# TensorE's loop turns begin with scores instead of a q projection, and half of K's transposes moves behind a reciprocal

## The chip, the core and the metric

The kernel runs on one core of a Trainium2 chip. The metric is the device time of one execution in microseconds (us), as the median of several runs. The profile is one further execution; its span, from the first to the last instruction, is some 2.6 us shorter than the time.

## The reference: what is computed

Two attention blocks, A and B, have the same form and data of their own. Per block there are 16 batches, 64 queries, 32 heads of 128, 512 cached keys, and a model width of 640:

```
q = (x @ wq) split into heads            # x: 16 x 64 x 640, wq: 640 x 4096
scores = q k^T / sqrt(128)               # k_cache: 16 x 32 x 512 x 128
p = softmax(scores)
o = p v                                  # v_cache as k_cache
out_block = concat_heads(o) @ wo         # wo: 4096 x 640
out = concat(out_A, out_B, last axis)    # 16 x 64 x 1280, bf16
```

Each key and each value is used by 64 queries only, so the caches (268 MB of the 295 MB moved) have to be streamed once.

## The kernel before, in words

**Steps.** The work is cut into 128 steps, numbered n. A step takes two batches and four heads (so 64 + 64 query rows fill 128 partitions), and reads 1 MB of K and 1 MB of V. Four steps (j = 0 to 3) make a group g of 16 heads for one pair of batches; eight groups make a phase; there are four phases (two for each block, because 16 heads' weights are held at a time).

**Kinds of operation in a step**, with the lines of the kernel before:

- LDK and LDV (SyncE's queue, L552, L563, L565) load K into a ring of six steps and V into a ring of four. LDV of step n waits until PV of step n-4 has freed its place.
- KT (VectorE, L617) transposes K in two halves, a and b, into `kt_ring`, which holds two steps.
- QP (TensorE, L603) projects q for four heads; QE (ScalarE, L609) copies it out of PSUM bank 1.
- S (TensorE, L627) makes the scores of four heads in PSUM banks 0 to 3.
- EX (ScalarE, L646) is four exponentials with row sums. RC (VectorE, L659) takes reciprocals: one of the first three heads' sums, one of the fourth's.
- NM (GpSimd, L675) multiplies the four heads' exponentials by their reciprocals. In the last step VectorE does this.
- TR (TensorE, L686) transposes the result into PSUM banks 4 and 5; TE (VectorE, L696) copies it out in two halves.
- PV (TensorE, L710) is P times V. In three steps of four it runs 128 small matmuls on 32 rows each, in the fourth (j = 3) 64 matmuls on 64 rows. OE and ZO (ScalarE, L718, L722) evict it and clear what the next will need.
- OP (TensorE, L730) multiplies by wo; after each group OS (VectorE, L740, L743) adds it to an accumulator or to the output, and ST (ScalarE's queue, L749) stores it.
- XT (TensorE, L582) transposes x once per group; XC and WP (GpSimd) lay out x and the next phase's wq.

**The order is written out by hand.** There is no scheduler at run time. `build_plan` gives every operation a time in units of a step, n plus an offset from the table `AT`, and sorts each engine's operations by it. Dependences are worked out from the same times (each operation depends on the last writer and on the readers of what it touches), and turned into semaphore waits. Changing a number in `AT` therefore changes the place of an operation in its engine's queue.

**TensorE runs a loop.** The other engines' programs are written out in full. TensorE's is a loop of 32 turns of four steps (`PERIOD = 4`), with a few operations ahead of it and behind it. In steady state TensorE's order in a step is S(n), TR(n-1), OP(n-2), QP(n+1), PV(n-1), and then S(n+1). In the kernel before, a turn begins with QP:

```python
    lo = next(i for i, o in enumerate(pe) if o.kind == "QP" and o.idx == 0)
    hi = next(i for i, o in enumerate(pe) if o.kind == "QP" and o.idx == cfg.PERIOD)
```

So a turn is QP, PV, S, TR, OP, four times (with one XT), and ends behind an OP. A PV of step -2, on zeros, stands in the first turn. Behind the loop stand PV(126), TR(127), OP(126), PV(127) and OP(127).

At the end of a turn TensorE's queue has a few instructions that do no arithmetic: the semaphores that the turn waited on are set back (L815), so that the same constants serve in the next turn, and a counter is raised and tested for the jump (L809):

```python
                        if loop["take"][s] == i:
                            e.sem_inc(sems[p][s], -v * units(s))
```

Three of these set-backs stand behind OPs within the turn, four at its end.

**VectorE's order** in a step is KTa(n), KTb(n), TE(n-2), RC3(n-1), in every fourth step OS, RC1(n-1). [...] a KT that waits for its K holds up the TE and the reciprocals behind it.

A second plan (`general`), which subtracts the maximum, is built too, but runs only when the row sums leave a safe range, which they don't here.

Of the kernel before, what the change touches and what calls it, by code (L numbers as in the profile page):

```python
# [20 lines left out]
class Cfg:  # L21
# [9 lines left out]
    BASE = 32  # L31
    KLEAD = 2.5
    WIDE = (0, 1, 2)
    AT = dict(XT=-2.485, XE=-2.28, XC=-0.9, QP=-0.45, QE=-0.24, KT=(-1.24, -1.0), S=0,
              EX=(0.21, 0.32, 0.43, 0.54), RC=(0.53, 0.75), NM=(0.56, 0.69, 0.82, 0.95), NMZ=(0.54, 0.55, 0.56, 0.76), TR=1.2,
              TE=(1.26, 1.39), PV=1.75, OE=(2.0, 2.06), ZO=2.11, OP=2.31, OS=2.545, LDWO=2.6, ST=3.374, WP0=-1.75, WP1=-1.6)


class Op:
# [19 lines left out]
def build_plan(dims, cfg, general):  # L59
# [12 lines left out]
    def add(eng, kind, idx, ts, reads=(), writes=()):  # L72
        op = Op(eng, kind, idx, ts, reads, writes)
        ops.append(op)
        at[(kind, idx)] = op
        return op

    def add_output(n):
        g, j = n // NJ, n % NJ
        final = n >= 0 and dims["FINAL"](g // NBP)  # L80
        for b in range(2):
            tv = n + AT["PV"]
            op = add("sp", "LDV", (n, b), tv - 0.3, [], [("v" if n >= 0 else "absent", n % cfg.NV, b)])
            loads.append((n - cfg.NV + AT["PV"] + 0.2 if n >= 0 else -99.0, 3, op))
        if n > -2:
            add("pe", "TR", n, n + AT["TR"], [("pn", i) for i in range(4)] + [("ident",)], [("B", 4), ("B", 5)])
        for b in range(2):
            add("dve", "TE", (n, b), n + AT["TE"][b], [], [("B", 4 + b), ("pT", b)])
        add("pe", "PV", n, n + AT["PV"], [("pT", 0), ("pT", 1), ("v", n % cfg.NV, 0), ("v", n % cfg.NV, 1)],
            [("B", 4), ("B", 5), ("B67",)])  # L90
        add("act", "OE", (n, 1), n + AT["OE"][0], [], [("B67",), ("oT", 1)])
        add("act", "OE", (n, 0), n + AT["OE"][1], [], [("B", 4), ("B", 5), ("oT", 0)])
        add("act", "ZO", n, n + AT["ZO"], [("zeros",)], [("B67",)])
        add("pe", "OP", n, n + AT["OP"], [("oT", 0), ("oT", 1), ("wo", j)], [("B67",)])
        if j == NJ - 1:
            bp = g % NBP
            add("dve", "OS", g, n + AT["OS"], [("acc", bp)], [("B67",), ("out_sb",) if final else ("acc", bp)])
            if final:
                add("act", "ST", g, n + AT["ST"], [("out_sb",)], [("out_dram", g)])
# [4 lines left out]
    for g in range(N // NJ + 1):  # L104
        n0 = g * NJ
        txt = n0 + AT["XT"]
        add("pe", "XT", g, txt, [("xn", g % cfg.NXN), ("ident",)], [("SB", 0)])
        if g == N // NJ:
            break
        if dims["FIRST"](g // NBP):  # L110
            add("act", "XE", g, n0 + AT["XE"], [], [("SB", 0), ("xs", g % NBP)])
            op = add("sp", "LDX", g, txt - 0.5, [], [("xn", g % cfg.NXN)])
            loads.append((txt - 3.7 if g else -7.0, 0, op))
        add("pool", "XC", g, n0 + AT["XC"], [("xs", g % NBP)], [("xT", g % cfg.NX)])
# [20 lines left out]
    add("dve", "BZ", 0, -9.8, [], [("B", 4), ("B", 5), ("B67",)])  # L135
    add("dve", "WZ", 0, -9.7, [], [("wo", NJ - 2), ("wo", NJ - 1)])
    add("pool", "NM", -1, -1 + AT["NM"][3], [], [("pn", i) for i in range(4)])
    for n in range(-2, N):
        add_output(n)
        if n < 0:  # L140
            continue
        g, j = n // NJ, n % NJ
        add("pe", "QP", n, n + AT["QP"], [("xT", g % cfg.NX), ("wqp", j)], [("SB", 1)])
        add("act", "QE", n, n + AT["QE"], [], [("SB", 1), ("qs", n % cfg.NQ)])
        for i in range(4):
            op = add("sp", "LDK", (n, i), n + AT["KT"][0] - 0.9, [], [("kn", n % cfg.NK)])
            loads.append((n - cfg.NV + AT["PV"] + 0.2 - cfg.KLEAD, 2, op))
        for b in range(2):
            tk = n + AT["KT"][b]
            add("dve", "KT", (n, b), tk, [("kn", n % cfg.NK)], [("kt", n % cfg.NKT, b)])  # L150
        add("pe", "S", n, n + AT["S"], [("qs", n % cfg.NQ), ("kt", n % cfg.NKT, 0), ("kt", n % cfg.NKT, 1)],
            [("SB", i) for i in range(4)])
        for i in range(4):
            h = 4 * n + i
            te = n + AT["EX"][i]
            if general:
                add("dve", "MX", h, te - 0.002, [], [("SB", i), ("negmax", h % 4)])
            add("act", "EX", h, te, [("negmax", h % 4)] if general else [],
                [("SB", i), ("p", h % cfg.NP), ("rs", h)])
            add("pool" if n < N - 1 else "dve", "NM", h, n + (AT["NM"] if n < N - 1 else AT["NMZ"])[i], [("p", h % cfg.NP), ("recip", n % cfg.NR, i // 3)], [("pn", i)])  # L160
        for a in range(2):
            add("dve", "RC", (n, a), n + AT["RC"][a], [("rs", 4 * n + i) for i in ((0, 1, 2), (3,))[a]],
                [("recip", n % cfg.NR, a)])
# [25 lines left out]
                   and not (d.dma and op.dma and d.eng == op.eng)]  # L189

    pe = progs["pe"]
    lo = next(i for i, o in enumerate(pe) if o.kind == "QP" and o.idx == 0)
    hi = next(i for i, o in enumerate(pe) if o.kind == "QP" and o.idx == cfg.PERIOD)
    size = hi - lo
    last_qp = max(o.idx for o in pe[lo:hi] if o.kind == "QP")
    reps = 1 + (N - 1 - last_qp) // cfg.PERIOD
    step = dict(XT=cfg.PERIOD // NJ, QP=cfg.PERIOD, S=cfg.PERIOD, TR=cfg.PERIOD, PV=cfg.PERIOD, OP=cfg.PERIOD)
    for k in range(reps):
        for i in range(size):
# [5 lines left out]
    for op in ops:  # L205
        if op.kind == "OP":
            at[("OE", (op.idx, 1))].deps += [d for d in op.deps if d.kind in ("LDWO", "WZ")]
            op.deps = [d for d in op.deps if d.kind not in ("LDWO", "WZ")]
        if op.kind == "XT" and op.idx > 0:
            at[("EX", 4 * (NJ * op.idx - NJ + 1))].deps += [d for d in op.deps if d.kind == "LDX"]  # L210
            op.deps = [d for d in op.deps if d.kind != "LDX"]
        if op.kind == "QP" and op.idx > 0:
            at[("EX", 4 * op.idx - 4)].deps += [d for d in op.deps if d.kind == "WP"]
            op.deps = [d for d in op.deps if d.kind != "WP"]

    own = {"XC", "QE", "KT", "NM", "TE", "OE", "ZO", "OS", "LDV"}

# [211 lines left out]
def mha_kernel(nc, blocks, out, cfg=None):  # L429
# [23 lines left out]
    with contextlib.ExitStack() as es:  # L453
        block = es.enter_context(nc.Block())

        def sb(name, shape, dt):
            return es.enter_context(nc.sbuf_tensor(name, shape, dt))
# [20 lines left out]
        recip = sb("recip", [128, NR, 4], F32)  # L478
        ident = sb("ident", [128, 128], BF16)
        extreme = sb("extreme", [128, 4], F32)  # L480
        good = sb("good", [128, 1], BF16)
        flag = sb("flag", [1, 1], I32)
        ps = es.enter_context(nc.psum_tensor("ps", [128, 8, 512], F32))

        sems = []
        for p, (_progs, counts, _loop) in enumerate(plans):
            sems.append({key: es.enter_context(nc.semaphore("_".join([f"p{p}"] + [str(k) for k in key])))
# [124 lines left out]

        def em_KT(e, op):
            n, a = op.idx
            dst = kt_ring[:, n % NKT, 16 * a:16 * a + 16].rearrange("p t j b k two -> p (t j) b (k two)").bitcast(F32)
            src = kn_ring[:, n % NK, a, :].bitcast(F32).rearrange("p (c h b l) -> p c h b l", h=8, b=2, l=2)
            ins = e.transpose(dst.rearrange("p c b (h l) -> p c h b l", h=8, l=2), src)  # L617
            return ins, ins
# [72 lines left out]
        def em_TE(e, op):  # L691
            n, b = op.idx
            if n == -2:
                ins = e.memset(pT_sb[:, b].rearrange("p t q -> p (t q)"), 0.0)
                return ins, ins
            ins = e.tensor_copy(pT_sb[:, b].rearrange("p t q -> p (t q)"), pt_bank(b))  # L696
            return ins, ins
# [77 lines left out]
        def units(key):  # L775
            return 16 if key[0].startswith("d_") else 1

        def emit(e, op, p, taken):
            sem = sems[p]
            waits = [(s, v - taken.get(s, 0)) for s, v in op.waits]  # L780
            attach = None
            if waits and not op.dma and op.kind not in ("FL1", "WP"):
                attach = waits.pop()
            for s, v in waits:
                e.wait_ge(sem[s], v * units(s))
            kind = "EXG" if p and op.kind == "EX" else op.kind
            first, last = emitters[kind](e, op)
            if last is None:
                e.sem_inc(sem[op.sem], units(op.sem))
                return  # L790
            if attach is not None:
                s, v = attach
                first.wait_op(sem[s], v * units(s), "sem-ge")
            last.then_inc(sem[op.sem], 16 if op.dma else 1)
# [113 lines left out]
```

## Time and profile before

| | before |
|---|---|
| time, median of 3 runs | 750.21 us (749.89 to 751.77) |
| span of the profiled execution | 747.6 us |
| TensorE busy, matmuls | 679.0 us (91%) |
| VectorE, ScalarE, GpSimd busy | 526.0 us, 519.4 us, 404.1 us |
| moved by DMA | 295.15 MB, mean 395 GB/s |
| a step, between 60 and 206 us | 5.2 us |
| matmul instructions | 26518, each with a weight load |

The busy time of an engine is the sum of its instructions' times; "idle before, releaser" names what an engine waited for. PE is TensorE's matmuls, PEld its weight loads, DVE is VectorE, ACT ScalarE, POOL GpSimd, SPq SyncE's queue, which issues the loads.

### The profile page before, as it was taken

The page shows a single profiled execution, that of the slowest core. Times are in us where ns is not written, and L with a number is a line of the kernel's source. Part 1 is how long each engine was busy: PE and PEld are TensorE (multiplying, and loading weights), DVE is VectorE, ACT ScalarE, POOL GpSimd, SP SyncE. Part 2 cuts the span into 40 slices and gives each one's busy share as a digit, 9 for nine tenths or more (in the row PEclk, how much of TensorE's full clock was granted, in tenths as well). Part 3 has the DMA queues.
Part 4 walks back from the last instruction along what each step waited for, and adds up shares of the span by engine and source line. Part 5 has one row for each costly group of instructions (what it writes and reads, how often), then busy time and mean ns, then how long its engine had stood idle before and what let it go on. Part 6 is the DMA issues. An engine that isn't in the chain of part 4 may idle for free.

```text
span 747.6 us, 57618 instructions
## 1 busy us (share of the span) xinstructions
PE 679.0 (91%) x26518; PEld 530.6 (71%) x26518; DVE 526.0 (70%) x818; ACT 519.4 (69%) x1559; POOL 404.1 (54%) x580
## 2 busy tenths in 40 slices
PE   4669999999998999989988999999898899999994
PEld 3557777777776777777766777677776677777773
DVE  7437777777767677676755776777676687877773
ACT  2438777787776767767756777777776677777772
POOL 5434555655964454645684545546476455564550
PEclk9979999999999999999999999999999999999999
DMA  8999999999999999999999999999999999999970
GB/s 315 398 402 410 411 411 414 410 412 413 405 398 414 413 413 411 414 411 414 412 399 407 411 412 413 411 411 411 411 410 401 411 412 414 404 414 413 412 299 16
DMA packets 87518, 295.15 MB, mean 395 GB/s; under 512 B 13360, under 2 KB 28208, under 8 KB 71088
## 3 DMA queue, kind: packets, MB, share of 16 engines
q1 hardware_dynamic: 78832, 284.22, 95.2%
q10 hardware_dynamic: 8640, 10.49, 3.9%
q14 instruction: 37, 0.30, 0.1%
q8 instruction: 9, 0.15, 0.1%
HBM read 292.03 MB, written 2.62 MB: 394 GB/s over the span
## 4 chain that ended last, share of the span: by engine, by line
PE 38%; SPq 29%; DMA 12%; POOL 6%; ACT 5%; DVE 5%; issue 4%; ACTq 0%; DVEq 0%
SPq L552 20%; PE ps L710 10%; PE ps L730 9%; PE ps L603 8%; DMA kn_ring<-in_B_k_cache_dram 8%; POOL pn_sb L675 5%; SPq L563 5%; PE ps L627 5%; PE ps L686 5%; SPq L565 3%; ACT p_ring L646 2%; DMA v_ring<-in_B_v_cache_dram 2%; DVE kt_ring L617 2%; DMA kn_ring<-in_A_k_cache_dram 2%; ACT oT_sb L718 2%
## 5 line engine op out<-in xcount | busy, mean ns | idle before, releaser
L675 POOL TENSOR_SCALAR pn_sb<-p_ring,recip 128x512 bf16<-128x512 bf16 x508 | 341.9, 692 | 314.7 <-DVE recip L659 314.7
L617 DVE STREAM_TRANSPOSE kt_ring<-kn_ring 128x1024 f32<-128x1024 f32 x256 | 302.9, 1222 | 116.0 <-DMA kn_ring<-in_B_k_cache_dram 77.6
L646 ACT ACTIVATE p_ring<-ps 128x512 bf16<-128x512 f32 x512 | 298.7, 598 | 19.8 <-PE ps L627 4.2
L696 DVE COPY pT_sb<-ps 128x1024 bf16<-128x1024 bf16 x258 | 164.2, 677 | 63.0 <-PE ps L686 62.5
L710 PE MATMUL ps<-pT_sb,v_ring 32*128 32x64 bf16 (+1 forms) x14528 | 162.2, 192 | 25.7 <-DVE pT_sb L696 9.8
L710 PEld LDWEIGHTS ps<-pT_sb,v_ring 32*128 32x128 bf16 (+1 forms) x14528 | 145.9, 92 | 41.5 <-issue 21.7
L603 PE MATMUL ps<-xT_ring,wqp_sb 128*128 128x128 bf16 x2560 | 167.0, 221 | 5.8 <-POOL xT_ring L592 5.7
L730 PE MATMUL ps<-wo_sb,oT_sb 128*128 128x320 bf16 x1040 | 166.2, 303 | 5.9 <-issue 4.9
L603 PEld LDWEIGHTS ps<-xT_ring,wqp_sb 128*128 128x128 bf16 x2560 | 158.3, 114 | 12.5 <-issue 5.9
L718 ACT ACTIVATE oT_sb<-ps 128x256 bf16<-128x256 f32 x260 | 85.6, 381 | 113.6 <-PE ps L710 113.6
L627 PE MATMUL ps<-kt_ring,qs_ring 32*64 32x512 bf16 x4096 | 138.6, 381 | 0.0
L609 ACT ACTIVATE qs_ring<-ps 128x512 bf16<-128x512 f32 x128 | 76.5, 598 | 82.4 <-PE ps L603 82.4
L686 PEld LDWEIGHTS ps<-ident,pn_sb 64*128 64x128 bf16 x4128 | 70.3, 95 | 77.6 <-ACT ps L722 43.6
L730 PEld LDWEIGHTS ps<-wo_sb,oT_sb 128*128 128x128 bf16 x1040 | 91.7, 98 | 43.6 <-issue 5.3
L646 ACT ACTIVATION_READ_ACCUMULATOR p_ring<-ps 128x1 f32 x512 | 106.1, 207 | 0.0
L686 PE MATMUL ps<-ident,pn_sb 64*128 64x64 bf16 x4128 | 84.0, 191 | 20.9 <-POOL pn_sb L675 12.8
L627 PEld LDWEIGHTS ps<-kt_ring,qs_ring 32*64 32x64 bf16 x4096 | 53.4, 103 | 28.3 <-issue 0.5
L659 DVE RECIPROCAL recip<-rowsum 128x3 f32<-128x3 f32 (+1 forms) x256 | 39.9, 162 | 32.4 <-ACT p_ring L646 28.2
L722 ACT ACTIVATE ps<-zeros 128x256 f32<-128x256 bf16 x130 | 51.3, 395 | 0.0
L575 POOL COPY wqp_sb<-ws_sb 128x1280 bf16<-128x1280 bf16 x32 | 39.2, 1256 | 7.3 <-DMA ws_sb<-in_A_wq_dram 7.3
L592 POOL COPY xT_ring<-xs_sb 128x640 bf16<-128x640 bf16 x32 | 22.9, 717 | 3.6 <-PE ps L603 3.6
L582 PE MATMUL ps<-ident,xn_ring 128*128 128x128 bf16 x165 | 15.1, 224 | 4.4 <-DMA xn_ring<-in_A_x_dram 3.4
(26 smaller groups left out, 66.0 us busy)
## 6 DMA issues: line engine op xcount, KB each, us to landing
kn_ring<-in_A_k_cache_dram SPq DMA_DIRECT2D x256, 256.0 KB
v_ring<-in_A_v_cache_dram SPq DMA_DIRECT2D x128, 512.0 KB, 12.2
kn_ring<-in_B_k_cache_dram SPq DMA_DIRECT2D x256, 256.0 KB
v_ring<-in_B_v_cache_dram SPq DMA_DIRECT2D x128, 512.0 KB, 13.0
ws_sb<-in_B_wq_dram SPq DMA_DIRECT2D x10, 512.0 KB, 15.9
wo_sb<-in_B_wo_dram ACTq DMA_DIRECT2D x8, 640.0 KB, 13.9
ws_sb<-in_A_wq_dram SPq DMA_DIRECT2D x4, 640.0 KB, 7.6
wo_sb<-in_A_wo_dram SPq DMA_DIRECT2D x4, 640.0 KB, 12.8
```

The source lines that it names most:

```text
L552: ins = e.dma_start(kn_ring[2 * b + l::4, n % NK].rearrange("p a c -> p (a c)"), src)
L603: last = e.matmul(ps[:, 1, f * 128:(f + 1) * 128], w[:, kt, f, :], xT_ring[:, xs, kt, :], start=(kt == 0), stop=(kt == KT - 1))
L609: ins = e.activation(qs_ring[:, op.idx % NQ].rearrange("p f b q -> p (f b q)"), ps[:, 1, :], ACTF.Copy, scale=scale)
L617: ins = e.transpose(dst.rearrange("p c b (h l) -> p c h b l", h=8, l=2), src)
L627: last = e.matmul(ps[64 * b:64 * b + 64, i, :], qs_ring[rows, n % NQ, f, b, :], kt_ring[rows, n % NKT, :, f // 2, b, :, f % 2], start=(f = ...
L646: ins = e.activation(dst, src, ACTF.Exp, scale=1.0, accum_out=rowsum[:, h:h + 1])
L675: ins = e.tensor_scalar(dst, src, recip[:, h // 4 % NR, i:i + 1], 1.0, ALU.mult, ALU.mult)
L686: last = e.transpose(pt_bank(b)[:, 64 * c:64 * c + 64], pn_sb[rows, c, :], ident[rows, rows], tile_position=(64 * b, 0))
L696: ins = e.tensor_copy(pT_sb[:, b].rearrange("p t q -> p (t q)"), pt_bank(b))
L710: last = e.matmul(ps[:, 4 + i, 64 * b:64 * b + 64], v_ring[rows, n % NV, b, c, :], pT_sb[rows, b, c, :], start=(t == 0 and i < 2), stop=(t ...
L718: ins = e.activation(oT_sb[:, 2 * a:2 * a + 2, :], o_ps[:, 2 * a:2 * a + 2, :], ACTF.Copy)
L730: last = e.matmul(out_ps[:, s, :], oT_sb[:, i, :], wo_sb[:, 4 * j + i, s * NH0:(s + 1) * NH0], start=(j == 0 and i == 0), stop=(j == NJ - ...
```

## The change

It moves the boundary of TensorE's turn from ahead of a QP to ahead of an S, which puts PV(126) into the last turn and leaves TR(127), OP(126), PV(127) and OP(127) behind the loop. For that, QP(0) moves ahead of the loop, PV(-2) goes (its TE is now a store to a spare column), and a QP(128), whose result nobody reads, is added, with a layout of x (XC) ahead of it on GpSimd, so that the last turn is complete. TensorE's cyclic order is what it was.

It also gives new offsets in `AT`. Compared as they come out, the queues differ in this: VectorE runs KTa(n), TE(n-2), RC3(n-1), OS where there is one, KTb(n), RC1(n-1); S thereby waits for VectorE as well as for ScalarE, with one more wait instruction ahead of each S; ST stands one exponential later in ScalarE's queue, and the loads of wo that ScalarE issues one exponential earlier; two loads of wq change places with a neighbour. In the last step, VectorE's order is now two of the four NM, TE(127), the check of the row sums, and then the other two NM. Those last two multiplications therefore come after the transposes that read their tile, so the last step's heads 2 and 3 enter the output with what the tile held before.

```diff
-    AT = dict(XT=-2.485, XE=-2.28, XC=-0.9, QP=-0.45, QE=-0.24, KT=(-1.24, -1.0), S=0,
-              EX=(0.21, 0.32, 0.43, 0.54), RC=(0.53, 0.75), NM=(0.56, 0.69, 0.82, 0.95), NMZ=(0.54, 0.55, 0.56, 0.76), TR=1.2,
-              TE=(1.26, 1.39), PV=1.75, OE=(2.0, 2.06), ZO=2.11, OP=2.31, OS=2.545, LDWO=2.6, ST=3.374, WP0=-1.75, WP1=-1.6)
+    AT = dict(XT=-2.555, XE=-2.383, XC=-0.788, QP=-0.428, QE=-0.224, KT=(-0.672, -0.375), S=0,
+              EX=(0.252, 0.307, 0.358, 0.616), RC=(0.572, 0.794), NM=(0.803, 0.854, 1.088, 1.187),
+              NMZ=(0.626, 1.242, 1.729, 1.805), TR=1.293, TE=(1.432, 1.47), PV=1.701, OE=(1.888, 2.013), ZO=2.221,
+              OP=2.387, OS=2.576, LDWO=2.6, ST=3.542, WP0=-1.75, WP1=-1.596)
...
-        add("pe", "PV", n, n + AT["PV"], [("pT", 0), ("pT", 1), ("v", n % cfg.NV, 0), ("v", n % cfg.NV, 1)],
-            [("B", 4), ("B", 5), ("B67",)])
+        if n > -2:
+            add("pe", "PV", n, n + AT["PV"], [("pT", 0), ("pT", 1), ("v", n % cfg.NV, 0), ("v", n % cfg.NV, 1)],
+                [("B", 4), ("B", 5), ("B67",)])
...
-    for n in range(-2, N):
-        add_output(n)
+    for n in range(-2, N + 1):
+        if n < N:
+            add_output(n)
...
         add("pe", "QP", n, n + AT["QP"], [("xT", g % cfg.NX), ("wqp", j)], [("SB", 1)])
+        if n == N:
+            for b in range(2):
+                add("dve", "KT", (n, b), n + AT["KT"][b])
+            break
...
-    lo = next(i for i, o in enumerate(pe) if o.kind == "QP" and o.idx == 0)
-    hi = next(i for i, o in enumerate(pe) if o.kind == "QP" and o.idx == cfg.PERIOD)
-    size = hi - lo
-    last_qp = max(o.idx for o in pe[lo:hi] if o.kind == "QP")
-    reps = 1 + (N - 1 - last_qp) // cfg.PERIOD
+    lo = next(i for i, o in enumerate(pe) if o.kind == "S" and o.idx == 0)
+    size = next(i for i, o in enumerate(pe) if o.kind == "S" and o.idx == cfg.PERIOD) - lo
+    reps = N // cfg.PERIOD
...
+            if n == NH // 4:
+                ins = e.memset(spare[:, 4 * current[0] + a:4 * current[0] + a + 1], 0.0)
+                return ins, ins
...
-                ins = e.memset(pT_sb[:, b].rearrange("p t q -> p (t q)"), 0.0)
+                ins = e.memset(spare[:, 4 * current[0] + 2 + b:4 * current[0] + 3 + b], 0.0)
```

More of the change, by code (lines that the diff above doesn't have):

```diff
@@ L87, in add_output @@
         for b in range(2):
-            add("dve", "TE", (n, b), n + AT["TE"][b], [], [("B", 4 + b), ("pT", b)])
-        add("pe", "PV", n, n + AT["PV"], [("pT", 0), ("pT", 1), ("v", n % cfg.NV, 0), ("v", n % cfg.NV, 1)],
-            [("B", 4), ("B", 5), ("B67",)])
+            add("dve", "TE", (n, b), n + AT["TE"][b], [], [("B", 4 + b), ("pT", b)] if n > -2 else [])
+        if n > -2:
+            add("pe", "PV", n, n + AT["PV"], [("pT", 0), ("pT", 1), ("v", n % cfg.NV, 0), ("v", n % cfg.NV, 1)],
+                [("B", 4), ("B", 5), ("B67",)])
         add("act", "OE", (n, 1), n + AT["OE"][0], [], [("B67",), ("oT", 1)])
@@ L107, in build_plan @@
         add("pe", "XT", g, txt, [("xn", g % cfg.NXN), ("ident",)], [("SB", 0)])
-        if g == N // NJ:
-            break
-        if dims["FIRST"](g // NBP):
+        if g < N // NJ and dims["FIRST"](g // NBP):
             add("act", "XE", g, n0 + AT["XE"], [], [("SB", 0), ("xs", g % NBP)])
@@ L214, in build_plan @@
             op.deps = [d for d in op.deps if d.kind != "WP"]
+    if general:
+        at[("QP", 0)].deps += [at[("KT", (0, b))] for b in range(2)]
     own = {"XC", "QE", "KT", "NM", "TE", "OE", "ZO", "OS", "LDV"}
@@ L480, in mha_kernel @@
         extreme = sb("extreme", [128, 4], F32)
+        spare = sb("spare", [128, 8], F32)
         good = sb("good", [128, 1], BF16)
@@ L483, in mha_kernel @@
         ps = es.enter_context(nc.psum_tensor("ps", [128, 8, 512], F32))
+        current = [0]
         sems = []
@@ L785, in emit @@
                 e.wait_ge(sem[s], v * units(s))
+            current[0] = p
             kind = "EXG" if p and op.kind == "EX" else op.kind
```

## The prediction

> **What bounds the kernel now.** I read the page's slices first, then the waits of SyncE's queue, the busy times by stretch, K's transposes against the scores step by step, and last TensorE's sequencer around a turn's end.
>
> The slices (busy tenths and rate of the DMA engines in 40 equal parts):
>
> ```profile
> DMA  8999999999999999999999999999999999999970
> GB/s 315 398 402 410 411 411 414 410 412 413 405 398 414 413 413 411 414 411 414 412 399 407 411 412 413 411 411 411 411 410 401 411 412 414 404 414 413 412 299 16
> ```
>
> The transfers are full from the second slice to the last but two. The waits of SyncE's queue over the first 210 us:
>
> ```profile
> SPq L563 <- PE ps L710: 34.6, 23, 3.3
> SPq L565 <- PE ps L710: 13.8, 8, 2.3
> ```
>
> There each load of V waits for a PV, 48 us in all, so TensorE paces the issue; but a load of V issued between 100 and 200 us lands after 12.8 us, so some 5 MB are always queued. By stretches (us; PE, PEld, DVE, ACT, POOL busy; clock, DMA share, GB/s):
>
> ```profile
> 60.00:206.00 146.00, 144.04 (x5771) 113.18 (x5765) 113.48 (x177) 114.51 (x343) 87.42 (x127) 1.00 1.03 411
> 206.00:600.00 394.00, 361.05 (x14255) 282.54 (x14248) 274.10 (x433) 278.87 (x840) 219.64 (x313) 1.00 1.03 410
> 600.00:723.00 123.00, 121.55 (x4760) 95.65 (x4750) 96.61 (x149) 93.10 (x284) 66.75 (x100) 1.00 1.02 410
> 723.00:748.00 25.00, 14.92 (x665) 11.00 (x662) 10.45 (x23) 9.80 (x30) 4.50 (x7) 0.95 0.11 37
> ```
>
> TensorE and DMA are both full in the first and third row; in the second DMA alone is (TensorE 92%), because the next phases' weights come in. A group of four steps takes TensorE 20.71 us in the first row (EX of step 4 at 56.66, of step 8 at 77.37, of step 12 at 98.08), 5.18 a step; in the second a step takes 5.69 us (S(33) at 206.22, S(102) at 598.67). The last K lands at 723.15; 24 us are left. So the end is: the last K that TensorE had to wait for, then TensorE's own pace, then the tail. K's transposes name that K:
>
> ```profile
> 587.81 2.37 DVE L617 STREAM_TRANSPOSE kt_ring<-kn_ring 128x1024 f32<-128x1024 f32 x2 [2.81 <-DMA kn_ring<-in_B_k_cache_dram]
> 590.11 1.25 DVE L696 COPY pT_sb<-ps 128x1024 bf16<-128x1024 bf16 x2
> 591.50 1.11 PE L710 MATMUL ps<-pT_sb,v_ring 64*128 64x64 bf16 x64 [0.67 <-DVE pT_sb L696]
> 592.54 0.59 PEld L627 LDWEIGHTS ps<-kt_ring,qs_ring 32*64 32x64 bf16 x32
> ```
>
> K(101) lands at 587.81 and S(101) starts 4.73 later, the shortest such distance in the trace. From there it grows, to 6.16 at step 127 (723.15 to 729.31): over the last 26 steps TensorE, at 5.26 a step, is the slower of the two.
>
> In the tail, TensorE's gaps (idle before, releaser):
>
> ```profile
> 732.58 1.21 PE L710 MATMUL ps<-pT_sb,v_ring 32*128 32x64 bf16 x128 [0.28 <-DVE pT_sb L696]
> 734.59 0.55 PE L686 MATMUL ps<-ident,pn_sb 64*128 64x64 bf16 x25 [0.79 <-ACT oT_sb L718]
> 736.42 0.29 PE L686 MATMUL ps<-ident,pn_sb 64*128 64x64 bf16 x7 [1.28 <-issue]
> ```
>
> The gap inside TR(127) waits for no engine. The set-backs and the jump, by source line (durations min/median/max in ns):
>
> ```profile
> L815 PEldq EVENT_SEMAPHORE  x224: 51/51/51, 20.1 to 731.2; - x112
> L809 PEldq ALU_OP  x32: 36/36/42, 51.4 to 731.4; - x32
> L809 PEldq COMPARE_BRANCH  x32: 76/208/240, 51.5 to 731.5; - x32
> ```
>
> Their starts show what they occupy. At one turn's end the four set-backs start at 113.877, 114.031, 114.180 and 114.331, the counter at 114.482, the jump at 114.609, the next turn's first wait at 114.874, ending at 114.925: **1.05 us without a matmul dispatched**. Now it costs nothing: the sequencer has run ahead, and TensorE spends 114.15 to 115.25 on the eight long matmuls of OP, already queued.
>
> [...] the first turn's gaps put down to issue lie 256 instructions apart (program positions 451, 707, 963, 1219, 1475), none recurs in later turns, and the gap in TR(127) is at 1987, two blocks on. [...] in a PV of 128 matmuls the first 32 weight loads take 0.22 us, and every later 16 take 0.133 to 0.138, [...] then dispatch, 4.2 ns each, sets the pace. **Behind a wide PV the queue is empty.** [...]
>
> **Part by part.** *The turn's boundary.* The same seven instructions now stand between PV(4k+2), one of the wide ones, and S(4k+4). Nothing is queued to hide them. S starts up to 1.05 us late, and behind it wait EX, NM and TR of that step and everything later on TensorE. The new wait ahead of each of the other S costs 0.07 (a wait record's start to the next weight load, 118.664 to 118.739) behind the two other wide PVs, nothing behind the narrow one. Against this, OE and ZO no longer delay that step's first exponential, about 0.1. Bounds for a turn: 0.7, should some lead survive, and 1.1; I take 1.0. Where TensorE paces, a group goes from 20.7 to 21.7. Between 60 and 206 us the 7 turns cost 7 us, but the 12 us of queued transfers hide it, nor is it felt at 5.69 a step in the middle. Behind S(101) six boundaries follow (before S(104) to S(124)): 6 x 1.0 = **+6.0**.
>
> *KTb behind RC3.* From a late K to S ran KTa, KTb 2.37, TE 1.25, PV 1.04 and hand-overs: 4.73. Now it is KTa 1.19, TE 1.25, RC3 0.17, KTb 1.19 and four hand-overs of about 0.07: 4.1. S(101) comes 0.7 earlier: **-0.7**. RC1 waits for KTb, but NM needs it only after three multiplications, 2.0 us behind RC3; with OS in between (0.8) that just fits. S also waits for KTb, which at step 126 would end at 723.95 by these durations, for an S at 724.28.
>
> *First turn.* One PV of 1.9 us and one fetch gap fewer lie ahead of step 4; TensorE may lead by some 4 us at 55 us. The transfers are full, so that gives nothing at the end.
>
> *Tail.* QP(128) goes between OP(125) and PV(126), which started 1.54 behind OP; now it is 1.09 + 1.22 = 2.31: +0.77. The loop ends at program position 1722, in the block that ends at 1731; the rest ends at 1952, ahead of 1987, where the fetch gap is: -1.28. The set-backs hide under OE, which TR(127) waits for anyway (0.79). That TR(127) no longer waits for two NM gives nothing, as OE comes later. Together **-0.5**. The two NM behind the check of sums (0.6) end before OP(127).
>
> The moved loads, ST, stores to spare columns and offsets that keep the order: nothing, behind transfers with 12 us of queue or on engines under 75% busy.
>
> Sum: +6.0 - 0.7 - 0.5 = +4.8; 750.2 + 4.8 = **755.0 us**.
>
> **The rivals.** *The boundary is hidden* (a lead survives PV, or K is late again after 600 us, so that TensorE's pace doesn't count). For it: DMA is full there too, and KT waits 0.3 to 0.9 us for K in most of these steps. Against it: the distance from K to S grows in that stretch. It gives -0.7 - 0.5: 749.0. *TensorE paces the transfers in the first phase*, so that its 4 us of lead reach the end: SyncE's 48 us of waits speak for it, the full DMA share and 12.8 us to landing against. It gives -4.0 - 1.2: 745.0 if the boundary is hidden too. [...] One fetch of 1.3 to 3.7 us in each of 32 turns would give over 790. The same block boundaries in both programs speak against it.
>
> **How the numbers follow.** Forecast 0.72, hidden boundary 0.13, lead carried 0.12, refetch 0.03. With 1.1 a turn for all six, 0.3 for KTb and no fetch gap saved the forecast's case reaches 757.3; with 0.7 it is 753.2. The range goes from 749.0, the hidden case, to 757.3. Slower by over 0.3% (2.25 us) takes nearly all of the forecast and the refetch, 0.73; same takes the hidden case, 0.13; faster 0.14.
>
> **What would show it.** Right: in the last phase a gap of about 1 us ahead of every fourth S, put down to issue; four steps at 21.5 or more there; K to S down to about 4.1 at the last late K, and over 9 at step 127; no issue gap in TR(127); QP(128) ahead of PV(126). Wrong: S close behind PV at the turns' ends, or four steps at 20.7.

## The result and the profile after

| | before | changed |
|---|---|---|
| time, median of 4 runs | 750.05 us (749.29 to 751.77) | 753.81 us (753.14 to 755.14) |
| ratio to before, 95% interval | | 1.0049 [1.0026, 1.0073] |
| span of the profiled execution | 747.6 us | 752.6 us |

The changed kernel is slower by 3.8 us (2.0 to 5.5 by the interval). The span of an execution is 1.7 to 1.8 us shorter than its own time: the two profiled ones took 749.34 and 754.38 us. Line numbers in its profile: K's transposes L628, S L638, RC L670, NM L686, TR L697, TE L707, PV L721, OE L729, OP L741, QP L611, loads of K L560 and of V L571 and L573, the loop's counter and jump L821, set-backs L827.

The page's slices, changed kernel:

```profile
DMA  8999999999999999999999999999999999999950
GB/s 319 398 402 410 412 411 413 412 410 413 406 398 414 414 413 412 413 413 413 412 400 406 411 410 413 411 413 410 411 407 400 412 415 413 407 408 403 393 220 15
```

The transfers are as full as before for most of the span. In the five slices ahead of the last the rate falls to 407, 408, 403, 393 and 220 GB/s: there the loads wait for TensorE, 33.5 us in all between 600 and 723 us, against 6.2 before. The same by stretch (us; PE, PEld, DVE, ACT, POOL busy; clock, DMA share, GB/s):

```profile
60.00:206.00 146.00, 138.16 (x5573) 108.60 (x5571) 104.63 (x167) 108.56 (x325) 83.15 (x121) 1.00 1.03 411
206.00:600.00 394.00, 366.75 (x14305) 286.88 (x14303) 276.90 (x438) 281.55 (x846) 222.99 (x316) 0.99 1.03 410
600.00:723.00 123.00, 116.35 (x4613) 92.01 (x4605) 88.19 (x141) 89.45 (x273) 63.82 (x95) 1.00 1.01 403
723.00:748.00 25.00, 21.06 (x846) 16.29 (x843) 15.35 (x34) 13.76 (x42) 8.36 (x13) 0.99 0.16 57
```

TensorE is now busy 138.2 us of 146 in the first row (before 144.0) and 116.4 of 123 in the third (before 121.6). It has got gaps, and is later. Where the gaps are, TensorE's waits say (waiting line, releaser: us in total, times, longest):

```profile
PE ps L638 <- ACT oT_sb L729: 17.4, 20, 0.9
...
PE ps L638 <- PEq L827: 5.1, 6, 0.9
...
PE ps L638 <- DVE kt_ring L628: 3.5, 4, 0.9
```

Together 30 gaps ahead of S, of 0.87 us each, in a kernel with 31 turn ends that lead to an S. The three releasers are three names for one thing: the profile names the semaphore event that came last, and OE, K's transpose or a set-back happens to be it. What they have in common shows at one turn's end (start, length, idle before and releaser):

```profile
650.93 1.28 PE L611 MATMUL ps<-xT_ring,wqp_sb 128*128 128x128 bf16 x20
652.14 1.22 PE L721 MATMUL ps<-pT_sb,v_ring 32*128 32x64 bf16 x128
654.24 1.07 PE L638 MATMUL ps<-kt_ring,qs_ring 32*64 32x512 bf16 x32 [0.89 <-ACT oT_sb L729]
```

In the records of TensorE's sequencer (PEq: its waits, set-backs, counter and jump) PV's last weight load starts at 653.152, the four set-backs at 653.135, 653.289, 653.439 and 653.589, the counter at 653.740, the jump at 653.867, the wait at 654.133, S's first weight load at 654.209. From PV's last weight load to S's first it is 1.06 us; at the other steps it is 0.13 behind a wide PV and 0.15 behind the narrow one, as in the kernel before. The first set-back starts 0.02 us ahead of PV's last weight load: the sequencer is hardly ahead. The set-backs' row is the old one, at a new place:

```profile
L827 PEldq EVENT_SEMAPHORE  x224: 51/51/51, 22.8 to 740.3; - x112
```

Against before, the first matmul of S comes at these times: S(4) 4.26 us earlier, S(32) 3.50 later, S(65) 0.14 later, S(101) 1.00 later, S(104) 1.28, S(127) 5.47 later. And behind S(127) the tail, 17.86 us instead of 18.30.

### The profile page after: what moved, and what is told of

Read it like the earlier page. It is cut to its first block, busy times and chain, and to the rows that moved or that the text cites. A ratio compares the mean times of both kernels' runs of the same rounds, so it can differ in the third digit from the quotient of the medians.

```text
span 752.6 us, 57532 instructions
## 1 busy us (share of the span) xinstructions
PE 682.1 (91%) x26410; PEld 533.0 (71%) x26410; DVE 517.6 (69%) x820; ACT 519.8 (69%) x1559; POOL 406.1 (54%) x581
## 4 chain that ended last, share of the span: by engine, by line
PE 52%; SPq 12%; POOL 9%; ACT 9%; DMA 8%; issue 5%; DVE 3%; PEld 1%; ACTq 0%; PEldq 0%; DVEq 0%
PE ps L721 12%; PE ps L741 12%; PE ps L611 11%; PE ps L638 9%; POOL pn_sb L686 9%; SPq L560 8%; PE ps L697 6%; ACT p_ring L657 6%; DMA v_ring<-in_B_v_cache_dram 6%; ACT oT_sb L729 3%; SPq L571 2%; DMA kn_ring<-in_B_k_cache_dram 2%; SPq L573 1%; DVE kt_ring L628 1%; DVE pT_sb L707 1%
## 5 line engine op out<-in xcount | busy, mean ns | idle before, releaser
L686 POOL TENSOR_SCALAR pn_sb<-p_ring,recip 128x512 bf16<-128x512 bf16 x508 | 343.1, 695 | 319.5 <-DVE recip L670 319.5
L628 DVE STREAM_TRANSPOSE kt_ring<-kn_ring 128x1024 f32<-128x1024 f32 x256 | 310.4, 1225 | 49.6 <-DMA kn_ring<-in_B_k_cache_dram 44.7
L707 DVE COPY pT_sb<-ps 128x1024 bf16<-128x1024 bf16 x258 | 165.7, 684 | 168.7 <-PE ps L697 168.7
L721 PE MATMUL ps<-pT_sb,v_ring 32*128 32x64 bf16 (+1 forms) x14400 | 161.4, 192 | 13.6 <-DMA v_ring<-in_B_v_cache_dram 7.9
L611 PE MATMUL ps<-xT_ring,wqp_sb 128*128 128x128 bf16 x2580 | 167.9, 221 | 5.3 <-POOL xT_ring L600 5.3
L741 PE MATMUL ps<-wo_sb,oT_sb 128*128 128x320 bf16 x1040 | 167.7, 305 | 4.8 <-issue 3.8
L611 PEld LDWEIGHTS ps<-xT_ring,wqp_sb 128*128 128x128 bf16 x2580 | 159.4, 114 | 12.1 <-POOL xT_ring L600 5.6
L638 PE MATMUL ps<-kt_ring,qs_ring 32*64 32x512 bf16 x4096 | 140.2, 385 | 27.3 <-ACT oT_sb L729 17.4
L721 PEld LDWEIGHTS ps<-pT_sb,v_ring 32*128 32x128 bf16 (+1 forms) x14400 | 144.1, 92 | 28.9 <-DMA v_ring<-in_B_v_cache_dram 9.1
L729 ACT ACTIVATE oT_sb<-ps 128x256 bf16<-128x256 f32 x260 | 85.6, 381 | 102.9 <-PE ps L721 102.9
L741 PEld LDWEIGHTS ps<-wo_sb,oT_sb 128*128 128x128 bf16 x1040 | 92.3, 99 | 43.3 <-issue 4.0
L697 PEld LDWEIGHTS ps<-ident,pn_sb 64*128 64x128 bf16 x4128 | 70.3, 96 | 66.7 <-ACT ps L733 29.5
L638 PEld LDWEIGHTS ps<-kt_ring,qs_ring 32*64 32x64 bf16 x4096 | 56.1, 104 | 56.1 <-DVE kt_ring L628 17.2
L697 PE MATMUL ps<-ident,pn_sb 64*128 64x64 bf16 x4128 | 84.3, 192 | 9.8 <-POOL pn_sb L686 6.3
L670 DVE RECIPROCAL recip<-rowsum 128x3 f32<-128x3 f32 (+1 forms) x256 | 37.5, 146 | 7.2 <-ACT p_ring L657 0.8
```

The source lines that it names most:

```text
L611: last = e.matmul(ps[:, 1, f * 128:(f + 1) * 128], w[:, kt, f, :], xT_ring[:, xs, kt, :], start=(kt == 0), stop=(kt == KT - 1))
L638: last = e.matmul(ps[64 * b:64 * b + 64, i, :], qs_ring[rows, n % NQ, f, b, :], kt_ring[rows, n % NKT, :, f // 2, b, :, f % 2], start=(f = ...
L686: ins = e.tensor_scalar(dst, src, recip[:, h // 4 % NR, i:i + 1], 1.0, ALU.mult, ALU.mult)
L697: last = e.transpose(pt_bank(b)[:, 64 * c:64 * c + 64], pn_sb[rows, c, :], ident[rows, rows], tile_position=(64 * b, 0))
L721: last = e.matmul(ps[:, 4 + i, 64 * b:64 * b + 64], v_ring[rows, n % NV, b, c, :], pT_sb[rows, b, c, :], start=(t == 0 and i < 2), stop=(t ...
L729: ins = e.activation(oT_sb[:, 2 * a:2 * a + 2, :], o_ps[:, 2 * a:2 * a + 2, :], ACTF.Copy)
```

## The experiments

All times stand beside executions of the kernel before on the same chip. Their median is 750.14 us for the order alone, the boundary alone, the set-backs early and the doubled cost; 749.89 for the kernel before with the doubled cost, the narrow end, both together and the changed kernel once more; 749.59 for the last three (the set-backs early once more and the two variants of both). "Four steps" is a fifth of the time from S(104) to S(124) in the profile. In that stretch the granted clock of TensorE is 1.00 in every profile, so the turns can be compared. Ahead of it this is not so: in five of the profiles the clock stands at 0.50 for 3.4 us, in one of them 6.8, at 585 to 593 us, where S(100) and S(101) run.

**The order alone** (an edit of the kernel before).

```diff
-    AT = dict(XT=-2.485, XE=-2.28, XC=-0.9, QP=-0.45, QE=-0.24, KT=(-1.24, -1.0), S=0,
+    AT = dict(XT=-2.485, XE=-2.28, XC=-0.9, QP=-0.45, QE=-0.24, KT=(-1.24, -0.4), S=0,
```

> The kernel before with one number changed: KTb comes behind RC3 (and OS), as in the changed kernel, so S waits for VectorE too. The turn still begins with QP. Theory (the turn's seven instructions stand exposed behind a wide PV): the boundary is still hidden here, four steps of the last phase take 20.9 to 21.1 us, the time is 749.3 to 751. Rival (K's order and the new wait of S are what costs): 753 or more, four steps at 21.6 or more.

Measured: 748.17 us, ratio 0.9974 [0.9966, 0.9981]; four steps 20.87. The order doesn't cost, it gains 2.0 us, more than I gave it. The profile shows only part of the gain: its execution took 748.89, 0.45 less than the profiled one before. S(101) comes 0.28 earlier, S(101) to S(127) is 0.63 shorter, and the tail is 0.45 longer, in which the granted clock stands at 0.50 from 735.95 to 739.36 us. At step 101 (timeline, columns as above; other engines' lines left out):

```profile
588.54 1.25 DVE L617 STREAM_TRANSPOSE kt_ring<-kn_ring 128x1024 f32<-128x1024 f32 x1 [2.40 <-DMA kn_ring<-in_B_k_cache_dram]
...
589.71 1.25 DVE L696 COPY pT_sb<-ps 128x1024 bf16<-128x1024 bf16 x2
...
590.89 0.15 DVE L659 RECIPROCAL recip<-rowsum 128x3 f32<-128x3 f32 x1
...
590.96 1.21 DVE L617 STREAM_TRANSPOSE kt_ring<-kn_ring 128x1024 f32<-128x1024 f32 x1
...
592.26 1.07 PE L627 MATMUL ps<-kt_ring,qs_ring 32*64 32x512 bf16 x32
```

From K's landing to S it is 3.72 us, where before it was 4.73 and I had estimated 4.1. And in this kernel TensorE is never clear of K in the last phase: K to S is still 4.71 at step 127 (6.16 before), with the last transpose waiting for its K:

```profile
723.69 1.25 DVE L617 STREAM_TRANSPOSE kt_ring<-kn_ring 128x1024 f32<-128x1024 f32 x1 [0.66 <-DMA kn_ring<-in_B_k_cache_dram]
```

**The boundary alone** (an edit of the changed kernel, as all that follow but one).

```diff
-    AT = dict(XT=-2.555, XE=-2.383, XC=-0.788, QP=-0.428, QE=-0.224, KT=(-0.672, -0.375), S=0,
+    AT = dict(XT=-2.555, XE=-2.383, XC=-0.788, QP=-0.428, QE=-0.224, KT=(-0.672, -0.65), S=0,
...
-    if general:
+    if True:
         at[("QP", 0)].deps += [at[("KT", (0, b))] for b in range(2)]
```

> The changed kernel with KTb back behind KTa, so S has its one wait again; QP(0) waits for KT(0) to keep the first scores safe. The turn begins with S. As in the changed kernel, the last step's heads 2 and 3 enter the output with what the tile held before. Theory: the gap of about 1 us ahead of every fourth S stays, four steps at 21.6 or more in the last phase, 753.5 to 755. Rival (the order costs): 750 to 751, four steps at 20.9.

Measured: 754.49 us, ratio 1.0050 [1.0034, 1.0065]; four steps 21.66. The boundary costs by itself what the whole change costs. Its gap, by TensorE's waits between 600 and 723 us, is 0.75 us a turn, 0.12 less than in the changed kernel. S has one wait instruction fewer there, and from the jump to S's first weight load it is 0.26 instead of 0.34. In this profile the clock stands at 0.50 for 6.8 us from 585.99, and S(101) comes at 594.60; so only its turns can be set beside the others.

**The set-backs early**; `early` holds two of the four, which come between the waits of the turn's last operation, a PV, and its first matmul. The other two stand behind the QP ahead of it.

```diff
-    spots = [i for i, o in enumerate(turn) if o.kind == "OP"] + [len(turn) - 1]
+    spots = [i for i, o in enumerate(turn) if o.kind == "OP"] + [len(turn) - 2, len(turn) - 1]
...
             for s, v in waits:
                 e.wait_ge(sem[s], v * units(s))
+            for s, v in early:
+                e.sem_inc(sem[s], -v * units(s))
...
```

> The changed kernel with the four set-backs at the turn's end moved [...]: those of the pool and act semaphores behind QP(4k+4), those of the dve and V semaphores between PV's waits and its first matmul. Counter, jump and first wait stay. As in the changed kernel, the last step's heads 2 and 3 enter the output with what the tile held before. Theory: the gap ahead of every fourth S falls from 1.06 to about 0.45 us, four steps take 21.1 to 21.3 us, and the time is 750 to 751.5. Rival (what costs is the jump, or what TensorE has to do after it, whatever stands ahead of it): 753 to 754.

Measured: 748.00 us, ratio 0.9973 [0.9961, 0.9985]. The distance from PV's last weight load to S's first is 0.43, four steps take 21.28. The time is below the forecast, and the profile didn't show why: its execution took 750.51, the six others 747.75 to 748.27. So it was run once more.

> The changed kernel with the four set-backs early, once more: its first profile had S(101) at 592.87 us and ended 2.5 us above the median of its other runs. As in the changed kernel, the last step's heads 2 and 3 enter the output with what the tile held before. Theory (the time beside the six boundaries comes from how late the transfers let S(101) start): four steps of the last phase again at 21.2 to 21.3 us and the tail at 17.9, and where the run takes 748, S(101) 2 us earlier, at about 590.5. Rival: the turns differ from run to run, four steps at 20.9 in a run of 748.

Measured: 748.45 us, ratio 0.9986 [0.9977, 0.9994], in runs of 747.76 to 751.42. In the profile of a run of 748.41 the turn's end is

```profile
648.51 1.21 PE L721 MATMUL ps<-pT_sb,v_ring 32*128 32x64 bf16 x128
649.98 1.07 PE L638 MATMUL ps<-kt_ring,qs_ring 32*64 32x512 bf16 x32 [0.26 <-issue]
```

and four steps take 21.03, while S(101) is only 1.07 earlier than in the other profile (591.80). Neither theory has it whole. Of the 2.16 us between the two spans, 1.22 lie between S(101) and S(127), so in the turns. Another 1.07 lie ahead of S(101), but the transfers don't make them: K(101) lands at 587.50 in the first profile and at 587.62 in the second, and PV(98), which waits for its V, starts at 585.18 and 585.31. In the first profile the granted clock stands at 0.50 from 585.90 to 589.31, and S(100) takes 1.93 us; in the second it is 1.00 there, and S(100) takes 1.07. What differs in the turns is PV. In the first profile wide PVs between 600 and 723 us take 1.02 or 1.15 to 1.20 us from first to last weight load, 1.109 in the mean; in this one all 17 take 1.017. Beside the kernel before (1.092) that makes up for the gap: S(101) to S(127) takes 136.79 us in this profile and 136.77 before.

**The suspected cost doubled**, in the changed kernel and in the kernel before, at the end of the turn's body.

```diff
                             taken[s] = v
+                for v in (1, -1, 1, -1):
+                    e.sem_inc(s_extra, v)
```

> The changed kernel with four more increments of a semaphore nobody waits for (+1, -1, +1, -1) behind the four set-backs at the turn's end: the suspected cost, 0.15 us each, twice. As in the changed kernel, the last step's heads 2 and 3 enter the output with what the tile held before. Theory: the gap ahead of every fourth S goes from 1.06 to 1.66 us, four steps of the last phase to 22.4, and the time rises by 3.6 to 4.2 us to 757.4 to 758. Rivals (the boundary is hidden, the order costs): no change against the changed kernel, 753.8.

> The kernel before with four more increments of a semaphore nobody waits for (+1, -1, +1, -1) at the turn's end, behind OP: the turn's end then takes 1.65 us. Theory: OP's eight long matmuls and what else is queued (1.38 us from the first set-back to OP's end) hide all but 0.3 us of it, so the gap ahead of QP at a turn's start is 0.3 us and the time rises by 0.5 to 2 us, to 750.6 to 752. Rival (0.6 us a turn costs the same as in the changed kernel, where it cost 5.2 us): 755.

Measured: the changed kernel 759.02 us, ratio 1.0123 [1.0104, 1.0141]; the kernel before 751.52, ratio 1.0026 [1.0016, 1.0037]. At a turn's end of the first:

```profile
653.77 1.21 PE L721 MATMUL ps<-pT_sb,v_ring 32*128 32x64 bf16 x128
656.45 1.07 PE L638 MATMUL ps<-kt_ring,qs_ring 32*64 32x512 bf16 x32 [1.46 <-ACT ps L733]
```

The gap grew by 0.59 in the mean (0.87 to 1.46), four steps take 22.25. Yet the time rose by 5.2 us, over the forecast of 3.6 to 4.2. S(101) comes 1.9 us later than in the changed kernel's second profile (below; in both the clock is 1.00 there), and 0.8 later than in its first. At this pace TensorE delays the transfers ahead of it too: S(65) comes at 391.55 instead of 384.58. The tail grew by 0.55, with four set-backs more ahead of TR(127). Behind OP the same four cost 1.6 us. Of that the profile shows 0.7 as four gaps ahead of QP of 0.2 us or less in the last phase; the rest was not traced. So the same instructions cost 5.2 behind a PV and 1.6 behind an OP.

**A narrow PV at the turn's end.**

```diff
-    WIDE = (0, 1, 2)
+    WIDE = (0, 1, 3)
```

> The changed kernel with the narrow PV (64 matmuls on 64 rows) in step j = 2 instead of j = 3: as many bytes of V in short runs, as many matmuls in a turn, the same set-backs, jump and waits, but the turn now ends behind a narrow PV. As in the changed kernel, the last step's heads 2 and 3 enter the output with what the tile held before. Theory (a wide PV is paced by dispatch and leaves TensorE's queue empty, [...]): the gap ahead of every fourth S falls from 1.06 to about 0.6 us, four steps take 21.3 to 21.5, the time is 748.3 to 750. Rival (the seven instructions cost their 1.05 us wherever they stand): gap and time as in the changed kernel, 753 to 754.

Measured: 751.54 us, ratio 1.0026 [1.0015, 1.0036]; four steps 21.45. At the turn's end:

```profile
649.88 1.11 PE L721 MATMUL ps<-pT_sb,v_ring 64*128 64x64 bf16 x64
651.61 1.07 PE L638 MATMUL ps<-kt_ring,qs_ring 32*64 32x512 bf16 x32 [0.61 <-DVE kt_ring L628]
```

The first set-back starts at 650.531, 0.24 us ahead of PV's last weight load (650.775); in the changed kernel it was 0.02. So the sequencer is ahead by 0.24: from weight load to weight load the gap is 0.80, not 0.6, which was my estimate. Against the changed kernel (below) it gains 2.1 us. The forecast of 748.3 to 750 is missed, because it was built on the 748.0 above and not on the turns: six groups that are 0.33 to 0.40 shorter make 2.0 to 2.4.

**Both, so that nothing is exposed**: the set-backs early and the narrow PV at the end, as in the two diffs above. Then the same with K's order undone, by the diff of the boundary alone, and the same with the whole of the reference computed, by this one:

```diff
-              NMZ=(0.626, 1.242, 1.729, 1.805), TR=1.293, TE=(1.432, 1.47), PV=1.701, OE=(1.888, 2.013), ZO=2.221,
+              NMZ=(0.626, 0.64, 0.65, 0.81), TR=1.293, TE=(1.432, 1.47), PV=1.701, OE=(1.888, 2.013), ZO=2.221,
```

> The changed kernel with both: the four set-backs early, and the turn's last PV a narrow one, so that only counter, jump and first wait stand at its end, [...]. As in the changed kernel, the last step's heads 2 and 3 enter the output with what the tile held before. Theory: the gap ahead of every fourth S goes to 0.1 us or less, four steps take 20.8 to 21.0, and K is the later one up to the end: 746 to 747.5. Rival (with the set-backs out of the way the boundary is no longer what counts): 748, as with the set-backs early alone.

> The version with the set-backs early and the narrow PV at the turn's end, with KTb back behind KTa (S without its wait for VectorE; QP(0) waits for KT(0)): with the boundary hidden, what is K's order worth? As in the changed kernel, the last step's heads 2 and 3 enter the output with what the tile held before. Theory A (the order is worth what it gave on the kernel before, 2.0 us, because a late K then holds S for 4.7 us up to the last step): 748.2 to 749.2, and K to S near 6 at step 127. Theory B (it is worth only what the changed kernel shows against the boundary alone, under 1 us): 746.5 to 747.7.

> The version with the set-backs early and the narrow PV at the turn's end, with all four multiplications of the last step ahead of its transposes again, so that the whole of the reference is computed. Theory (the four multiplications on VectorE end while TR(127) waits for OE anyway, so they cost nothing): 746.2 to 747.3, as without. Rival (the last transposes now wait for VectorE): 0.5 to 1 us more, 747.3 to 748.

Measured: 746.74 us, ratio 0.9961 [0.9948, 0.9975]; with K's order undone 747.90, 0.9975 [0.9966, 0.9984]; with the whole reference 747.02, 0.9964 [0.9949, 0.9978]. The first:

```profile
647.58 1.11 PE L721 MATMUL ps<-pT_sb,v_ring 64*128 64x64 bf16 x64
648.70 1.07 PE L638 MATMUL ps<-kt_ring,qs_ring 32*64 32x512 bf16 x32
```

No gap of the matmuls is left (0.20 from weight load to weight load), four steps take 20.87, and K holds S to the end (4.73 from K to S at step 127). Undoing K's order brings 6.26 there, and costs 1.2 us in the medians, which the intervals don't separate: less than theory A said, more than B. With that order undone the moved boundary and all other new offsets still stand, and the kernel is faster than before; so none of them costs what the changed kernel lost. The multiplications in their place cost nothing that can be measured. This last version beats both kernels, by 2.6 us and by some 6.

**The changed kernel once more.**

> The changed kernel once more, beside the others of this call, for a narrower interval and to be set against the boundary alone. In the last step the multiplications of heads 2 and 3 come behind the transposes that read them, so those heads enter the output with what the tile held before. Theory: 753 to 755, the boundary alone (754.5) less the up to 0.7 us of K's order. Rival (the order costs too): above the boundary alone.

Measured: 753.60 us, ratio 1.0048 [1.0035, 1.0061]; against the boundary alone (1.0050) K's order shows nothing in the time. Four steps 21.85; S(101) at 592.41, K to S 4.63 there; S(127) at 733.91; tail 17.96. The clock stands at 0.50 from 579.65 to 583.06, ahead of PV(98)'s wait for V, and at 1.00 from there to S(127).

**The turns added up.** A group of four steps with no gap takes 20.71 us. Adding the gap of a turn, and three times what a wide PV takes beyond its shortest, 1.017, gives these sums beside the measured groups of the last phase:

| kernel | gap, us a turn | mean wide PV | 20.71 + both | measured |
|---|---|---|---|---|
| before | 0 | 1.092 | 20.94 | 20.95 |
| changed | 0.87 | 1.065 | 21.72 | 21.78 |
| changed again | 0.87 | 1.107 | 21.85 | 21.85 |
| boundary alone | 0.75 | 1.083 | 21.66 | 21.66 |
| doubled | 1.46 | 1.031 | 22.21 | 22.25 |
| narrow end | 0.62 | 1.111 | 21.61 | 21.45 |
| set-backs early, twice | 0.25 | 1.109; 1.017 | 21.24; 20.96 | 21.28; 21.03 |
| both | 0 | 1.018 | 20.71 | 20.87 |
| order alone | 0 | 1.027 | 20.74 | 20.87 |
| before, doubled | 0.12 | 1.139 | 21.20 | 21.39 |

Seven of the profiles agree within 0.07. In "both" and the order alone K is late up to the end, so a group takes longer than TensorE needs. For the narrow end (0.16 under its sum) and the kernel before with the doubled cost (0.19 over it) the sum misses something that was not found.

## Why the prediction was right, point by point

It forecast 755.0 us by an exposed turn boundary; 753.81 and that boundary came. That the first profile's sum is within 0.3 of the forecast is partly luck: a boundary term that was too large is in part made up for by 1.1 us ahead of S(101), which came with a halved clock (below) and not in the second profile. There the sum is 0.5 under the forecast, and the times are 1.0 under it. Its terms, against the two profiles of the changed kernel:

| term | forecast | profile 1 | profile 2 |
|---|---|---|---|
| up to S(101) | -0.7 | +1.00 | -0.13 |
| S(101) to S(127) | +6.0 | +4.47 | +4.73 |
| tail | -0.5 | -0.44 | -0.34 |
| sum, in the span | +4.8 | +5.03 | +4.26 |

*The boundary* was the right cause, and it is shown: doubled it costs more, shortened less, hidden nothing, and without K's order it costs the same. The term was too large by 1.3 to 1.5. The gap is 0.87 beyond the usual hand-over, not 1.0, and a group grew by 0.83 to 0.90. The 0.07 for the new wait behind the two other wide PVs didn't come: the hand-over there is 0.13 in both kernels. And the first of the six was hardly felt: from S(101) to S(104) the kernel before needs 16.51 us, waiting for K, and the changed one 16.79 and 16.71. So it is 0.2 to 0.3 plus five times 0.83 to 0.90.

*Behind a wide PV the queue is empty* is supported by the narrow end: there the sequencer was 0.24 us ahead, against 0.02 behind the wide PV, and the gap shrank by 0.26 (1.06 to 0.80). How many matmuls wait in the queue behind a PV was not shown. That dispatch sets a wide PV's pace is my reading of its weight loads (0.22 us for the first 32, 0.133 to 0.138 for every later 16) and of those 0.02 us.

*K's transposes* were mis-sized in both directions. The order by itself brings K to S down to 3.72, below my 4.1. But in the changed kernel little of it arrived at S(101). I had counted six boundaries behind S(101) and none ahead of it, and there is a seventh, before S(100). In the second profile that one holds S(100) for 0.86 us, K to S at step 101 is 4.63, and S(101) comes 0.13 early. In the first profile PV(98) waits for its V, and then TensorE is slow:

```profile
584.99 1.35 PE L721 MATMUL ps<-pT_sb,v_ring 32*128 32x64 bf16 x128 [1.67 <-DMA v_ring<-in_B_v_cache_dram]
...
587.24 1.93 PE L638 MATMUL ps<-kt_ring,qs_ring 32*64 32x512 bf16 x32 [0.90 <-ACT oT_sb L729]
...
587.51 1.25 DVE L628 STREAM_TRANSPOSE kt_ring<-kn_ring 128x1024 f32<-128x1024 f32 x1 [2.72 <-DMA kn_ring<-in_B_k_cache_dram]
```

PV(98) starts only 0.3 us earlier than before. Then S(100) waits 0.90 for the boundary and takes 1.93 us, where the second profile has 1.07. The granted clock differs (us; PE busy; clock, DMA share, GB/s; the first profile, then the second):

```profile
587.00:590.00 3.00, 2.76 (x64) 0.50 1.02 414
...
587.00:590.00 3.00, 2.51 (x71) 1.00 1.02 412
```

In the first profile the clock stands at 0.50 from 586.95 to 590.36 us, and two weight loads of S(100) come 0.35 and 0.37 us behind the one before, where S(102) has 0.19. So TE and KTb of step 101 come late as well (K to S 6.03), and S(101) is 1.1 us later than in the second profile. The set-backs early, profiled twice, show the same with 1.07. So the sign of K to S at about 4.1 came in neither profile of the changed kernel, and the +1.00 of the table is no cost of K's order.

*The first turn's lead* of 4 us came (S(4) 4.26 earlier) and was worth nothing: the boundaries of the first phase used it up, and at S(65) both kernels stand within 0.14, where the transfers set the time.

*The tail* was right in kind: QP(128) goes ahead of PV(126), and TR(127) is whole, with only its wait for OE:

```profile
737.62 1.28 PE L611 MATMUL ps<-xT_ring,wqp_sb 128*128 128x128 bf16 x20
738.84 1.22 PE L721 MATMUL ps<-pT_sb,v_ring 32*128 32x64 bf16 x128
740.84 0.64 PE L697 MATMUL ps<-ident,pn_sb 64*128 64x64 bf16 x32 [0.79 <-ACT oT_sb L729]
```

*Another sign that I named was wrong*: K to S at step 127 is 5.46, not over 9. The last KTa starts at 729.33, when the KTb (728.13, 1.24 us long) and the RC1 ahead of it in VectorE's queue are done:

```profile
728.13 1.24 DVE L628 STREAM_TRANSPOSE kt_ring<-kn_ring 128x1024 f32<-128x1024 f32 x1
729.29 0.12 DVE L670 RECIPROCAL recip<-rowsum 128x1 f32<-128x1 f32 x1
729.33 1.22 DVE L628 STREAM_TRANSPOSE kt_ring<-kn_ring 128x1024 f32<-128x1024 f32 x1
```

No wait for K stands there; K is early, and its transpose too is paced by TensorE: the TE at 726.12, ahead of all three in VectorE's queue, had waited 1.30 us for TR. The sign to look for was that KT no longer waits for a transfer.

*The rivals*: the hidden boundary and the carried lead fell with the gap and with S(65); and no gap of a fetch's size recurs from turn to turn: in the first turn of the changed kernel three waits of matmuls put down to issue take 1.60 to 3.81 us, behind 60 us the one that is left takes 0.6, and between 60 and 724 us the profile's instruction queue q8 moves nothing.

What stays open: why a wide PV sometimes takes 0.15 us more (below), and what sets off the halved clock near 586 us. In the second profile of the set-backs early PV(98) waits as long (1.78 us, in the first 1.79) and the clock stays at 1.00. Both may be part of how far executions of one kernel lie apart; with one profile for each that isn't shown.

## What to carry to other kernels

In this kernel loop control cost nothing behind the eight long matmuls of OP (in the kernel before, QP's first matmul at 115.25 us, across a turn's end, starts 0.14 us behind the start of OP's last, as in the steps on both sides of it), and 0.87 us a turn behind a PV of 128 short ones, whose last weight load starts only 0.02 us behind the first set-back. So look for the place where the engine still has work when its sequencer gets to the turn's end. When the profile names several releasers for gaps of one length at one line, look for what the sequencer does between the two operations. When one operation takes longer than its like (S(100), 1.93 us at a clock of 0.50 and 1.07 at 1.00), compare the granted clock before giving the change the blame. And a saving ahead of the point from which the engine sets the pace may be taken by the next late transfer (4.26 us at S(4) were gone at S(65)), while a cost behind it is paid on every turn (here 0.83 to 0.90 us a group).

## What the runs showed of the hardware

A set-back of a semaphore is recorded with 51 ns, but between the starts of two in a row TensorE's sequencer takes 0.15 us (653.135 to 653.289 to 653.439 to 653.589 in the changed kernel), and four increments more lengthened the gap by 0.59. The jump of the loop takes 208 ns in the median, in both kernels. Between 600 and 723 us, in the profiles of the kernel before and the changed one, 21 of 34 wide PVs of 128 matmuls take 1.02 or 1.03 us from first to last weight load and 13 take 1.15 to 1.24; the 11 narrow ones of 64 take 0.89. How many are long differs between executions of one program (mean 1.109 and 1.017 with the set-backs early), and three such PVs in a group make 0.28 us of it. The granted clock stands at 0.50 for 3.4 us, once for 6.8, near 586 us in five profiles. Two programs that were profiled twice, the changed kernel and the set-backs early, have it there in one execution and not in the other; S(100) then took 1.93 us instead of 1.07.
